# Row tiles transposed on TensorE, and a filtered spectrum laid out class by class

## The chip, the core and the metric

The kernel runs on one core of a Trainium2 chip. The metric is device time in microseconds (us) from start to end of one execution; lower is better. Its engines are TensorE (PE, matrix multiplication into PSUM; its loads of weights are listed as PEld), VectorE (DVE), ScalarE (ACT), GpSimd (POOL) and SyncE (SP), whose queue issues nearly all DMAs here. They run side by side, and each works through its own list in order.

## The reference

A normalised input goes through two branches, whose results are added to the input. Branch A is a filter in the frequency domain (a real two-dimensional FFT over 2048 rows and 640 columns, a product with a complex filter, the inverse), branch B a gated linear unit.

```python
xn = _layernorm(x, axis=-1)                  # x: 1 x 2048 x 640, bf16
X = jnp.fft.rfft2(xn.astype(jnp.float32))    # 2048 x 321
y = jnp.fft.irfft2(X * (w_r + 1j * w_i), s=(2048, 640)).astype(jnp.bfloat16)
h = (xn @ w_gate) * (xn @ w_up)              # 2048 x 1536
out = x + y + h @ w_down
```

## The kernel before

The 2048 rows are taken as 16 tiles of 128 rows and 640 columns. Everything lies in one SBUF tensor, `arena`, and one PSUM tensor, `ps`, of eight banks; so the profile names only these two, and the stages are told apart by line.

- **Layer norm.** Each tile's mean and variance come either from DVE (two L754, then L761) or from ACT (a sum L736, a sum of squares L745); `act_set` and `act_stats` say which tile goes where. ACT takes the root (L770, L771), DVE the reciprocal (L778) and the scaling in place (L795, named `mul`).
- **Transposes.** The gated unit needs the rows with their columns on the partitions. Tiles 0 to 3 are transposed on PE, five 128x128 blocks each (L814, named `T0`), and copied out of PSUM by ACT or DVE (`eT0`; L681 and L682 are the lines of all such copies on ACT and on DVE). Tiles 4 to 15 are transposed by a DMA each (L802, `xt`).
- **Gated unit.** `GU` multiplies by gate and up weights: L973 for tiles 0 and 1 singly (128 columns) and 2 and 3 together (256), L951 for four tiles at once (512 columns, 440 matmuls). The results are copied out (L681, L682) and multiplied on DVE (L991, L993).
- **Forward FFT.** DVE's butterflies over the columns (L857 to L892, `S1` to `S5`) feed a matmul `R` (L905). Then `D` (L1034) transforms within classes of columns, which are residues modulo ten, paired into four classes and one more for the multiples of five; `C` (L1053) finishes the rows.
- **Filter.** `WM` multiplies the spectrum in PSUM by the filter's real and imaginary parts: four L1070 for the four classes and one L1073 for the fifth, for each of 16 steps. `SM` (L1086, L1087) combines the products. `JA` to `JD` (L682, L681, L1099, L1100) write copies with real and imaginary parts exchanged.
- **Inverse.** `IA` (L1116), `I` (L1144), butterflies `V1` to `V5` (L1168 to L1201), and `IV` (L1233), which adds into the same PSUM bank as the down product.
- **Down product.** `ACC` (L1221, 396 matmuls) accumulates the gated unit's output; L1260 and L1242 add the input, and the rows are stored.

The order is not made while the kernel runs. Every piece of work is a task with what it reads and writes, and a table, `_PLAN`, lists for every task its engine and PSUM bank. Each engine runs its tasks in the table's order, and waits are derived from the dependences and from who held the bank before. The numbers given to tasks as durations serve only that bookkeeping. PE begins with `nwarm` matmuls on constants (L714) while the first tile is loaded and normalised.

In the filtered spectrum `L`, each of four groups holds 640 elements in which a class's elements lie four apart, and `IA` reads its weights so:

```python
yl = v_l[:, lr, o_ + 128 + k:o_ + 640:4] if k < 4 else v_l[:, lr, o_:o_ + 128]
```

Of the kernel before, what the change touches and what calls it, by code (L numbers as in the profile page):

```python
# [255 lines left out]
def _build_tables():  # L256
    t = {}
# [7 lines left out]
    for tt in range(16):  # L265
        for g in range(_G):
            q = tt * _G + g
# [14 lines left out]
    b = np.arange(64)  # L282
# [18 lines left out]
    l_ = 5 * np.arange(65)  # L301
    e = np.exp(-1j * two_pi * ((b[:, None] * l_[None, :]) % _D) / _D)
    w = np.where((l_ == 0) | (l_ == 320), 1.0, 2.0)[:, None] / _D * np.conj(e).T
    for o in range(2):
        own = (l_ % 2 == o).astype(np.float64)
        fd[64 * o:64 * o + 64, 512:577] = e.real * own[None, :]
        fd[64 * o:64 * o + 64, 578:641] = (e.imag * own[None, :])[:, 1:64]
        gd[63:128, 512 + 64 * o:576 + 64 * o] = w.real * own[:, None]
        gd[0:63, 512 + 64 * o:576 + 64 * o] = -(w.imag * own[:, None])[1:64]
# [59 lines left out]
_LP = 321  # L369
_YS = 1090  # L370
# [30 lines left out]
def _d_act(n):  # L401
# [4 lines left out]
    (12, 1, -1), (19, 2, -1), (10, 0, 1), (0, 3, -1), (11, 4, -1), (13, 4, -1), (18, 2, -1), (20, 2, -1), (28, 2, -1),  # L406
    (27, 2, -1), (170, 1, -1), (14, 4, -1), (8, 3, -1), (21, 1, -1), (22, 2, -1), (29, 2, -1), (23, 2, -1), (30, 1, -1),
    (31, 2, -1), (32, 2, -1), (24, 0, 3), (25, 2, -1), (26, 2, -1), (9, 0, 7), (33, 0, 1), (34, 2, -1), (35, 2, -1),
    (181, 0, 0), (182, 2, -1), (36, 1, -1), (37, 1, -1), (15, 4, -1), (43, 1, -1), (38, 1, -1), (169, 4, -1), (179, 0, 6),
    (180, 2, -1), (39, 2, -1), (40, 2, -1), (183, 2, -1), (44, 1, -1), (45, 1, -1), (46, 2, -1), (47, 2, -1), (189, 0, 1),  # L410
    (191, 0, 0), (190, 1, -1), (192, 1, -1), (193, 2, -1), (172, 4, -1), (186, 0, 6), (171, 4, -1), (112, 2, -1), (187, 1, -1),
    (41, 0, 2), (42, 1, -1), (184, 0, 7), (185, 1, -1), (16, 4, -1), (54, 2, -1), (113, 2, -1), (48, 0, 6), (49, 1, -1),
    (62, 1, -1), (194, 0, 5), (196, 0, 3), (197, 1, -1), (195, 1, -1), (188, 2, -1), (198, 2, -1), (50, 2, -1), (51, 2, -1),
    (53, 2, -1), (114, 2, -1), (55, 2, -1), (52, 2, -1), (63, 1, -1), (206, 0, 2), (207, 1, -1), (64, 1, -1), (204, 0, 7),
    (205, 1, -1), (115, 2, -1), (173, 4, -1), (209, 0, 6), (174, 4, -1), (65, 1, -1), (210, 1, -1), (66, 1, -1), (67, 2, -1),
    (56, 1, -1), (57, 2, -1), (116, 2, -1), (199, 0, 3), (200, 1, -1), (70, 2, -1), (201, 0, 2), (202, 1, -1), (203, 2, -1),
    (58, 2, -1), (208, 2, -1), (17, 4, -1), (121, 2, -1), (72, 1, -1), (1, 4, -1), (211, 0, 7), (175, 4, -1), (212, 1, -1),
    (176, 4, -1), (177, 4, -1), (73, 1, -1), (117, 0, 2), (118, 1, -1), (119, 0, 5), (74, 1, -1), (213, 2, -1), (122, 2, -1),
    (68, 2, -1), (123, 2, -1), (75, 1, -1), (76, 1, -1), (77, 2, -1), (216, 0, 1), (217, 1, -1), (214, 0, 0), (215, 1, -1),
    (218, 2, -1), (221, 0, 2), (222, 1, -1), (78, 2, -1), (124, 2, -1), (219, 0, 3), (220, 1, -1), (223, 2, -1), (80, 2, -1),  # L420
    (224, 0, 4), (120, 1, -1), (225, 1, -1), (82, 1, -1), (60, 2, -1), (226, 0, 2), (227, 1, -1), (229, 0, 6), (230, 1, -1),
    (83, 1, -1), (84, 1, -1), (178, 4, -1), (231, 0, 5), (125, 2, -1), (128, 0, 6), (126, 0, 3), (129, 1, -1), (232, 1, -1),
    (228, 2, -1), (130, 2, -1), (233, 2, -1), (131, 2, -1), (59, 4, -1), (71, 4, -1), (2, 4, -1), (236, 0, 0), (237, 1, -1),
    (61, 4, -1), (85, 1, -1), (234, 0, 2), (127, 1, -1), (86, 1, -1), (235, 1, -1), (238, 2, -1), (132, 2, -1), (92, 1, -1),
    (241, 0, 6), (242, 1, -1), (239, 0, 7), (240, 1, -1), (93, 1, -1), (243, 2, -1), (133, 2, -1), (87, 2, -1), (246, 0, 4),
    (244, 0, 1), (245, 1, -1), (94, 1, -1), (247, 1, -1), (248, 2, -1), (134, 2, -1), (69, 4, -1), (249, 0, 6), (250, 1, -1),
    (95, 1, -1), (96, 1, -1), (97, 2, -1), (251, 0, 2), (252, 1, -1), (90, 2, -1), (253, 2, -1), (88, 2, -1), (98, 2, -1),
    (100, 2, -1), (254, 0, 7), (255, 1, -1), (256, 0, 3), (257, 1, -1), (438, 4, -1), (433, 4, -1), (259, 0, 4), (260, 1, -1),
    (258, 2, -1), (137, 0, 5), (139, 0, 0), (437, 4, -1), (435, 4, -1), (441, 4, -1), (472, 4, -1), (101, 4, -1), (91, 4, -1),
    (434, 4, -1), (470, 4, -1), (3, 4, -1), (135, 0, 2), (136, 1, -1), (143, 2, -1), (138, 1, -1), (102, 1, -1), (261, 0, 7),  # L430
    (262, 1, -1), (79, 4, -1), (89, 4, -1), (141, 0, 3), (269, 0, 2), (263, 2, -1), (142, 1, -1), (140, 1, -1), (266, 0, 5),
    (267, 1, -1), (144, 2, -1), (270, 1, -1), (264, 0, 4), (265, 1, -1), (268, 2, -1), (145, 2, -1), (271, 0, 5), (274, 0, 1),
    (103, 1, -1), (104, 1, -1), (272, 1, -1), (273, 2, -1), (81, 4, -1), (442, 4, -1), (466, 4, -1), (146, 2, -1), (105, 1, -1),
    (106, 1, -1), (275, 1, -1), (279, 0, 4), (280, 1, -1), (276, 0, 0), (277, 1, -1), (278, 2, -1), (107, 2, -1), (147, 2, -1),
    (110, 2, -1), (108, 2, -1), (468, 4, -1), (469, 4, -1), (281, 0, 6), (282, 1, -1), (286, 0, 7), (287, 1, -1), (283, 2, -1),
    (284, 0, 3), (152, 0, 4), (148, 0, 6), (153, 1, -1), (99, 4, -1), (431, 4, -1), (440, 4, -1), (432, 4, -1), (4, 4, -1),
    (683, 4, -1), (109, 4, -1), (111, 4, -1), (473, 4, -1), (156, 2, -1), (429, 4, -1), (439, 4, -1), (467, 4, -1), (471, 4, -1),
    (149, 1, -1), (285, 1, -1), (288, 2, -1), (157, 2, -1), (150, 0, 0), (289, 0, 2), (151, 1, -1), (154, 0, 4), (291, 0, 6),
    (296, 0, 0), (290, 1, -1), (292, 1, -1), (155, 1, -1), (293, 2, -1), (158, 2, -1), (301, 0, 2), (299, 0, 6), (300, 1, -1),
    (294, 0, 4), (295, 1, -1), (304, 0, 7), (306, 0, 6), (6, 4, -1), (297, 1, -1), (298, 2, -1), (159, 2, -1), (160, 2, -1),  # L440
    (305, 1, -1), (307, 1, -1), (309, 0, 0), (310, 1, -1), (302, 1, -1), (303, 2, -1), (311, 0, 7), (312, 2, -1), (308, 2, -1),
    (163, 0, 5), (164, 1, -1), (167, 0, 1), (161, 0, 3), (162, 1, -1), (168, 2, -1), (314, 0, 0), (315, 2, -1), (313, 2, -1),
    (165, 0, 4), (316, 0, 6), (317, 2, -1), (166, 1, -1), (446, 0, 2), (447, 1, -1), (448, 2, -1), (474, 0, 0), (443, 0, 4),
    (444, 2, -1), (445, 1, -1), (324, 0, 7), (325, 1, -1), (477, 0, 2), (479, 1, -1), (478, 2, -1), (318, 2, -1), (321, 0, 6),
    (322, 1, -1), (436, 4, -1), (451, 0, 4), (452, 2, -1), (475, 1, -1), (476, 1, -1), (449, 0, 2), (450, 2, -1), (498, 4, -1),
    (503, 4, -1), (504, 4, -1), (497, 4, -1), (534, 4, -1), (453, 2, -1), (319, 0, 7), (320, 1, -1), (323, 2, -1), (454, 2, -1),
    (326, 0, 6), (327, 1, -1), (328, 2, -1), (505, 0, 4), (506, 1, -1), (508, 0, 0), (509, 1, -1), (510, 1, -1), (331, 0, 7),
    (332, 1, -1), (334, 0, 2), (335, 1, -1), (329, 0, 6), (507, 1, -1), (482, 0, 0), (483, 2, -1), (480, 0, 2), (481, 2, -1),
    (484, 2, -1), (455, 1, -1), (330, 1, -1), (341, 0, 7), (342, 1, -1), (336, 0, 4), (337, 1, -1), (456, 3, -1), (457, 3, -1),
    (460, 0, 5), (462, 0, 6), (463, 1, -1), (458, 0, 0), (464, 0, 7), (465, 1, -1), (461, 1, -1), (344, 0, 1), (345, 1, -1),  # L450
    (536, 0, 6), (459, 1, -1), (537, 1, -1), (339, 0, 2), (538, 1, -1), (340, 1, -1), (349, 0, 1), (532, 4, -1), (500, 4, -1),
    (499, 4, -1), (502, 4, -1), (501, 4, -1), (511, 0, 3), (333, 2, -1), (485, 2, -1), (531, 4, -1), (565, 4, -1), (535, 4, -1),
    (560, 4, -1), (530, 4, -1), (528, 4, -1), (529, 4, -1), (513, 0, 6), (351, 0, 0), (486, 2, -1), (350, 1, -1), (352, 1, -1),
    (512, 2, -1), (567, 0, 1), (568, 1, -1), (569, 1, -1), (346, 0, 5), (347, 1, -1), (487, 3, -1), (488, 3, -1), (489, 0, 4),
    (490, 1, -1), (514, 2, -1), (338, 2, -1), (515, 2, -1), (354, 0, 0), (355, 1, -1), (539, 0, 2), (540, 1, -1), (541, 1, -1),
    (493, 0, 1), (491, 0, 6), (492, 1, -1), (494, 2, -1), (356, 0, 4), (357, 1, -1), (359, 0, 7), (360, 1, -1), (517, 2, -1),
    (343, 2, -1), (516, 2, -1), (495, 0, 2), (5, 4, -1), (430, 4, -1), (533, 4, -1), (544, 0, 0), (594, 4, -1), (561, 4, -1),
# [887 lines left out]
```

## Time and profile before

| what | value |
|---|---|
| median of 3 runs (lowest to highest) | 196.71 us (196.61 to 196.75) |
| the profiled execution | 196.57 us |
| its span, first to last instruction | 194.9 us |
| PE busy | 190.9 us, 98% |
| DVE busy | 176.7 us, 91% |
| ACT busy | 136.4 us, 70% |
| POOL busy | 12.2 us, 6% |
| mean DMA rate | 122 GB/s, 23.73 MB |
| DMA transposes | 12, issued 19.6 to 58.6 us, 3.8 us median to landing |
| chain that ended last | PE 95%, DVE 2%, DMA 1%, ACT 1% |

The profile is of one execution. A group row gives line, engine, operation, what is written from what, the shape and the count; after the bar, the busy time of the group, the mean duration of one in ns, and the idle time of the engine before it. A matmul's recorded end is modelled and overlaps the next, so the time from one start to the next says more than a duration. The chain follows, from the last instruction back, what each step waited for.

### The profile page before, as it was taken

What the parts mean: (1) busy time and instruction counts of PE and PEld (TensorE: products, weight loads), DVE (VectorE), ACT (ScalarE), POOL (GpSimd) and SP (SyncE); (2) the same over time, 40 slices, a digit from 0 to 9 for tenths busy, and PEclk for the clock granted to TensorE, in tenths of its full rate; (3) what the DMA queues carried; (4) which work ended last, traced back from release to release, by engine and by line L of the source; (5) the groups of instructions that cost most, each with busy time, mean ns of one, the idle gap of its engine ahead of it and who ended that gap; (6) DMA issues with size and microseconds to landing.
All of it is one profiled execution on the core that took longest, in us unless ns stands there. A gap on an engine that the chain in (4) does not pass through costs nothing.

```text
span 194.9 us, 4074 instructions
## 1 busy us (share of the span) xinstructions
PE 190.9 (98%) x1568; PEld 120.5 (62%) x1568; DVE 176.7 (91%) x369; ACT 136.4 (70%) x275; POOL 12.2 (6%) x22
## 2 busy tenths in 40 slices
PE   8899999999999999999999999999999999999995
PEld 8797454454454565555655555557777777777774
DVE  3899999999999999999989999987999999999713
ACT  3899999999884679989999999667305523253130
POOL 1000000000000000331031221120000000000000
DMA  5999974016869921366465510005001543135412
GB/s 173 324 370 324 214 98 111 0 37 105 155 130 222 258 68 27 96 145 193 118 153 135 153 36 31 3 0 170 4 0 53 144 143 104 40 95 172 134 68 67
DMA packets 29666, 23.73 MB, mean 122 GB/s; under 512 B 10448, under 2 KB 27600, under 8 KB 29520
## 3 DMA queue, kind: packets, MB, share of 16 engines
q1 hardware_dynamic: 28848, 23.08, 46.5%
q10 hardware_dynamic: 800, 0.41, 0.7%
q8 instruction: 12, 0.20, 0.5%
q14 instruction: 6, 0.05, 0.1%
HBM read 18.89 MB, written 2.62 MB: 110 GB/s over the span
## 4 chain that ended last, share of the span: by engine, by line
PE 95%; DVE 2%; DMA 1%; ACT 1%; issue 0%
PE ps L951 48%; PE ps L1221 27%; PE ps L973 5%; PE ps L1116 3%; PE ps L1034 2%; PE ps L1053 2%; PE ps L905 2%; PE ps L1144 2%; PE ps L1233 2%; DMA arena<-in_A_x_dram 1%; DVE arena L754 1%; PE ps L814 1%; ACT arena L681 1%; DVE arena L682 0%; DVE arena L761 0%
## 5 line engine op out<-in xcount | busy, mean ns | idle before, releaser
L681 ACT ACTIVATE arena<-ps 128x512 bf16<-128x512 f32 (+5 forms) x211 | 111.3, 582 | 48.8 <-PE ps L1233 13.8
L951 PE MATMUL ps<-arena 128*128 128x512 bf16 x440 | 101.9, 379 | 0.0
L951 PEld LDWEIGHTS ps<-arena 128*128 128x128 bf16 x440 | 40.9, 98 | 43.1 <-ACT arena L681 0.9
L1221 PE MATMUL ps<-arena 128*128 128x320 bf16 (+2 forms) x396 | 57.2, 295 | 0.0
L1221 PEld LDWEIGHTS ps<-arena 128*128 128x128 bf16 x396 | 37.6, 98 | 13.2
L1070 DVE TENSOR_TENSOR arena<-ps,arena 128x256 bf16<-128x256 f32 x64 | 22.6, 414 | 1.5 <-PE ps L1053 1.3
L991 DVE TENSOR_TENSOR arena<-arena 128x512 bf16<-128x512 bf16 x44 | 18.7, 426 | 0.6 <-ACT arena L681 0.2
L1260 DVE TENSOR_TENSOR arena<-arena 128x640 bf16<-128x640 bf16 x15 | 7.0, 486 | 5.4 <-ACT arena L681 5.4
L682 DVE CAST arena<-ps 128x512 bf16<-128x512 f32 (+4 forms) x16 | 10.1, 639 | 1.5 <-PE ps L973 0.4
L745 ACT ACTIVATE arena<-arena 128x640 bf16<-128x640 bf16 x12 | 10.2, 849 | 0.1
L682 POOL COPY arena<-arena 64x252 bf16<-64x252 bf16 x8 | 4.1, 510 | 92.8 <-DVE arena L1087 92.5
L973 PE MATMUL ps<-arena 128*128 128x128 bf16 (+1 forms) x120 | 9.5, 237 | 0.3 <-DVE arena L682 0.3
L1116 PEld LDWEIGHTS ps<-arena 128*128 128x128 bf16 x160 | 7.9, 116 | 3.0
L736 ACT ACTIVATE arena<-arena 128x640 bf16<-128x640 bf16 x12 | 9.0, 753 | 0.2
L973 PEld LDWEIGHTS ps<-arena 128*128 128x128 bf16 x120 | 8.4, 98 | 1.1 <-issue 0.4
L1100 POOL TENSOR_SCALAR arena<-arena 64x252 bf16<-64x252 bf16 x8 | 7.5, 943 | 22.9 <-DVE arena L1087 22.6
L1116 PE MATMUL ps<-arena 128*128 128x64 bf16 x160 | 8.3, 198 | 0.0
L1233 PE MATMUL ps<-arena 128*128 128x320 bf16 (+2 forms) x33 | 8.3, 295 | 0.0
L1034 PEld LDWEIGHTS ps<-arena 128*128 128x128 bf16 x160 | 6.4, 98 | 2.7 <-issue 0.5
L857 DVE TENSOR_TENSOR arena<-arena 128x768 f32<-128x768 bf16 (+1 forms) x10 | 7.9, 789 | 0.0
L1073 DVE TENSOR_TENSOR arena<-ps,arena 128x260 bf16<-128x260 f32 x16 | 6.9, 432 | 0.0
L1034 PE MATMUL ps<-arena 128*128 128x64 bf16 (+1 forms) x160 | 6.9, 193 | 0.0
(61 smaller groups left out, 184.3 us busy)
## 6 DMA issues: line engine op xcount, KB each, us to landing
arena<-in_A_x_dram SPq DMA_DIRECT2D x19, 160.0 KB, 2.6
arena<-in_A_w_i_dram SPq DMA_DIRECT2D x30, 80.2 KB, 2.3
arena<-in_A_w_r_dram SPq DMA_DIRECT2D x30, 80.2 KB, 2.3
out_dram<-arena SPq DMA_DIRECT2D x15, 160.0 KB, 1.9
arena<-in_B_w_gate_dram SPq DMA_DIRECT2D x4, 320.0 KB, 6.5
arena<-in_A_x_dram SPq DMA_DIRECT2D x1, 1280.0 KB, 10.8
arena<-c_tf SPq DMA_DIRECT2D x4, 256.0 KB, 4.6
arena<-c_ti SPq DMA_DIRECT2D x2, 512.0 KB, 5.0
```

What stands on the lines that cost most here:

```text
L681: return c.e.activation(dst, src, _ACTF.Copy)
L682: return c.e.tensor_copy(dst, src)
L736: return c.e.activation(v_jk, v_x[:, b, :], _ACTF.Copy, scale=1.0 / _D, accum_out=v_m32[:, b:b + 1])
L745: return c.e.activation(v_jk, v_x[:, b, :], _ACTF.Square, scale=-1.0, bias=v_m32[:, b:b + 1], accum_out=v_ss[:, b:b + 1])
L951: ins = c.e.matmul(ps[:, bk, :], v_gw[:, w, j, ft, :], v_xt[:, j, rows], start=(j == 0), stop=(j == 4))
L973: ins = c.e.matmul(ps[:, bk, i * n:(i + 1) * n], v_gw[:, w, j, ft0 + i, :], v_xt[:, j, rows], start=(j == 0), stop=(j == 4))
L991: return c.e.tensor_tensor(v_ht[:, ft0, rows], gb[:, 0, :], gb[:, 1, :], _OP.mult)
L1034: ins = c.e.matmul(ps[:, bk + i, k * 64:k * 64 + n], v_uq[:, k, t + i, :], v_fd[:, k * 128 + w * n: k * 128 + w * n + n], start=True, stop ...
L1070: c.e.tensor_tensor(dst, xh, wv, _OP.mult)
L1116: ins = c.e.matmul(ps[:, bk, 64 * k:64 * k + 64], yl, v_ti[:, q, 0, :], start=True, stop=True)
L1221: ins = c.e.matmul(ps[:, bk, 0:sl3.stop - sl3.start], v_ht[:, ft, a * 128:(a + 1) * 128], v_wd[:, ft, sl3], start=(ft == _FT_ORDER[0]), st ...
L1233: return c.e.matmul(ps[:, bank_of(own), 0:sl3.stop - sl3.start], v_sm[:, 2, :], v_v[:, a, sl3], start=False, stop=True)
```

## The change

1. The branch that issued a DMA transpose is gone; all 16 tiles go through `T0` and `eT0`. That makes 60 more 128x128 matmuls on PE, nine more tile copies on ACT, three more on DVE and twelve DMAs fewer on SP.
2. The products and the filtered spectrum are laid out class by class. In the products every class has a row of `_LB` = 66 elements, so that L1070 writes neighbouring results 66 elements apart. In `L` every class has 128 contiguous elements, which `IA` reads as they lie. The combine runs over 20 rows of 66 instead of four of 321; the two unused elements at the end of a row are cleared once by POOL. The fifth class's table in the inverse is reordered to match.
3. Tile 1's statistics go to ACT and tile 2's to DVE, `nwarm` is 43 instead of 42, and `_PLAN` is a new table. The constants' load for `R` stands earlier in SP's queue; of the inverse's copies out of PSUM four move from ACT to DVE; the order of tasks on each engine is new throughout.

```diff
+_LB = 66
...
 _PLAN = (
...
-        b_pr = alloc("PR", 8 * 321)
-        b_l = alloc("L", 2 * 2624)
+        b_pr = alloc("PR", 8 * 5 * _LB)
+        b_l = alloc("L", 2 * 2560)
...
-        v_pr = V("PR").rearrange("p (w g n) -> p w g n", w=2, g=4)
-        v_l = V("L").rearrange("p (r n) -> p r n", r=2)
+        v_pr = V("PR").rearrange("p (w g b c) -> p w g b c", w=2, g=4, b=5)
+        v_l = V("L").rearrange("p (r g b c) -> p r g b c", r=2, g=4, b=5)
...
-        nwarm = opts.get("nwarm", 42)
+        nwarm = opts.get("nwarm", 43)
...
-        aset = set(opts.get("act_set", (2, 3))) | set(range(opts.get("act_stats", 6), 16))
+        aset = set(opts.get("act_set", (1, 3))) | set(range(opts.get("act_stats", 6), 16))
...
-                if b >= opts.get("xt_dma", 4):
-                    def em_xt(c, b=b):
-                        return c.e.dma_start_transpose(v_xt[:, :, b * 128:(b + 1) * 128], v_x[:, b, :])
-                    T("xt%d" % b, "sp", 1330.0, em_xt, reads=[(b_x, ("s", b, b + 1))],
...
-                    continue
...
-                        dst = v_pr[:, w, 2 * pb:2 * pb + 2, 65:321].rearrange("p g (h m k) -> p h g m k", h=2, k=4)[:, h]
+                        dst = v_pr[:, w, 2 * pb:2 * pb + 2, 1:5, 32 * h:32 * h + 32].rearrange("p g k m -> p g m k")
                         c.e.tensor_tensor(dst, xh, wv, _OP.mult)
...
-                d5 = v_pr[:, :, 2 * pb:2 * pb + 2, 0:65]
+                d5 = v_pr[:, :, 2 * pb:2 * pb + 2, 0, 0:65]
                 return c.e.tensor_tensor(d5, x5, wt[:, :, :, 0:321:5], _OP.mult)
+            if t == 0:
+                def em_pad(c):
+                    return c.e.memset(v_pr[:].rearrange("p w g b c -> p (w g b) c")[:, :, 64:_LB], 0.0)
+                T("pad", "pool", 300.0, em_pad, writes=[(b_pr, None)], prio=pq - 0.002)
...
-                pa_, pb_ = v_pr[:, 0], v_pr[:, 1]
-                l_ = v_l[:, lr, 63:2623].rearrange("p (g n) -> p g n", g=4)[:, :, 0:321]
+                pa_, pb_ = (v_pr[:, w].rearrange("p g b c -> p (g b) c") for w in range(2))
+                l_ = v_l[:, lr].rearrange("p g b c -> p (g b) c")[:, :, 0:_LB]
...
-                src = l0[:, :, 1:64] if five else l0[:, :, 65:321]
-                dst = l1[:, :, 0:63] if five else l0[:, :, 321:577]
+                src = v_l[:, lr, :, 0, 1:64] if five else v_l[:, lr, :, 1:5, 0:64]
+                dst = v_l[:, lr, :, 0, 65:128] if five else v_l[:, lr, :, 1:5, 64:128]
...
-                        yl = v_l[:, lr, o_ + 128 + k:o_ + 640:4] if k < 4 else v_l[:, lr, o_:o_ + 128]
+                        yl = v_l[:, lr, q % 4, (k + 1) % 5]
```

## The prediction

> **What bounds the kernel now.** I read the page's busy shares first, then the chain that ended last in order of time, then the waits of TensorE (PE).
>
> ```profile
> PE 190.9 (98%) x1568; PEld 120.5 (62%) x1568; DVE 176.7 (91%) x369; ACT 136.4 (70%) x275; POOL 12.2 (6%) x22
> ```
>
> ```profile
> 40.67 0.84 PE ps L905 x15
> ...
> 42.87 10.79 PE ps L951 x50
> ...
> 75.10 0.59 PE ps L1034 x20
> ...
> 81.64 0.67 PE ps L1116 x20
> ...
> 138.95 6.66 PE ps L1221 x49
> ```
>
> A busy share alone proves little, because matmuls overlap. The chain rows (start us, length us, what) give the step from one matmul to the next: 10.79/50 = 0.216 us for 512 columns, 6.66/49 = 0.136 for 320, 0.84/15 = 0.056 for 128. These lie on one line (0.416 ns a column), so each is a rate and not a wait in disguise. With these steps, from L973's start at 7.31 us to the end of the last matmul (about 192.5), I add up: L951 440 x 0.2158 = 94.95; L1221 372 x 0.136 + 12 x 0.0825 + 12 x 0.056 = 52.3; L1233 4.3; L973 80 x 0.056 + 40 x 0.109 = 8.8; L814 0.6; L905 4.5; L1144 4.5; L1034 160 x 0.0296 = 4.7; L1053 32 x 0.137 = 4.4; L1116 160 x 0.0335 = 5.4. That is 184.4 us of matmul in a stage of 185.2 us. **PE's own work is the bound; only 0.8 us of waiting is left in it.** PE's listed waits all end by 7.31. DVE is full too, but beside PE:
>
> ```profile
> 10.00:60.00 50.00, 50.00 (x330) 27.60 (x328) 49.96 (x110) 46.11 (x104) 0.00 (x0) 1.00 0.71 155
> 60.00:130.00 70.00, 69.91 (x605) 38.26 (x604) 66.70 (x148) 61.57 (x110) 11.63 (x16) 1.00 0.44 110
> ```
>
> Columns: window, then busy PE, PEld, DVE, ACT, POOL, the granted clock (1.00), DMA. Spare are 3.9 us of ACT in the first window, 3.3 of DVE and 8.4 of ACT in the second.
>
> **The change part by part.** The profiled execution took 196.57 us (span 194.9 and 1.7 around it), 0.14 below the median of the runs, 196.71; I add the terms to 196.71.
>
> *Twelve tiles transposed on PE.* The old four show the price:
>
> ```profile
> 10.10 0.44 PE L814 MATMUL ps<-arena 128*128 128x128 bf16 x5
> 10.38 0.72 PE L973 MATMUL ps<-arena 128*128 128x128 bf16 x10
> ...
> 10.94 0.44 PE L814 MATMUL ps<-arena 128*128 128x128 bf16 x5
> ...
> 11.22 3.46 PE L973 MATMUL ps<-arena 128*128 128x128 bf16 x40
> ```
>
> PE goes on 0.28 us after each group of five starts: 12 x 0.28 = **+3.36 us**, all on the bound. No gap can hide it, since only 0.8 us of gaps exist. The Trainium skill ("TensorE: Matmul & The Clock Gate", Part 4) gives about 275 ns for one transpose in a kernel and says that the full clock does not engage for it. By that the sixty would be 16.5 us and the estimate 212.8; the rows above, 56 ns each, decide against it.
>
> They add waits to PE's queue: each group waits for its tile's scaling on DVE (L795), and ready GLU matmuls (L951) stand behind it. The first, tile 6, is the tightest: DVE ends group 0's butterflies at about 16.5 us (5.5 us of rows L857 to L892 and two 0.2 products from 10.4), then four statistics 1.6, aggregates and reciprocals 0.3, three scalings 1.1 and two products 0.7 make 20.2. PE reaches it at 12.65 + 4.36 (L973) + 3 x 1.08 (L951) + 2 x 0.28 (L905) = 20.8. So it waits for nothing, by 0.6.
>
> What leaves is twelve transposing DMAs (L802, 1.2 to 2.6 us each on SP's queue, 3.8 us median to landing). PE never waited for them, so this gains nothing; the filter loads that were queued behind them start earlier, which no PE wait asks for either.
>
> *Their evictions.* Nine more 640-element bf16 evictions on ACT and three on DVE. ACT's two of before took 0.72 each, 0.58 start to start: 9 x 0.58 = 5.3 us. Between 10 and 70 us ACT has 3.9 + 3.4 = 7.3 spare, so they fit, closely. On DVE 3 x about 0.4 = 1.2 in a stretch with none spare; but the class stage (L1034) also starts later by the PE time put ahead of it (eleven groups, 3.1 us), and that is room for the butterflies that feed it. Nothing on the path; if the cover fails, PE waits for a bank or for normalised rows (rival C).
>
> *Class by class layout.* The inverse matmul L1116 read its weights in steps of four elements; now they are contiguous. Same matmul size, contiguous weights: L1034.
>
> ```profile
> L1116 PEld LDWEIGHTS ps<-arena 128*128 128x128 bf16 x160 | 7.9, 116 | 3.0
> ...
> L1034 PEld LDWEIGHTS ps<-arena 128*128 128x128 bf16 x160 | 6.4, 98 | 2.7 <-issue 0.5
> ```
>
> The chain gives 33.5 ns a matmul against 29.5: 160 x 4 ns = **-0.64 us**. Ends: 0 and -0.64; I take the latter, as L1034 differs in nothing else that the rows show.
>
> The products are on DVE:
>
> ```profile
> 72.73 1.41 DVE L1070 TENSOR_TENSOR arena<-ps,arena 128x256 bf16<-128x256 f32 x4
> 74.05 0.43 DVE L1073 TENSOR_TENSOR arena<-ps,arena 128x260 bf16<-128x260 f32 x1
> ```
>
> Until now L1070 wrote runs of four neighbouring elements; now each element is written 66 from the last. No row of before writes so. Nearest: L1070 itself reads PSUM 64 elements apart, and L1073 reads its filter five apart. Both lie on the line of the f32 copies (256 elements 414 ns, 260 432, 512 689: about 1.02 ns an element), so hopping reads cost nothing; I take **0** for hopping writes. The slowest nearby row is POOL's copy, 510 ns for 252 elements, 2.02 ns each: +1.0 x 256 x 64 = 16.4 us of DVE as the upper end; the lower end, two elements a cycle as in L991 (512 in 426 ns), -8 us, off the path. Here the skill speaks against the change: "Vector Engine (DVE) Microarchitecture Reference", section 5.2, measures 1.71 to 2.51 ns a column instead of 1.05 where only the output hops every element, on 4-byte words. For 256 x 64 columns that would be 10.8 to 23.9 us of DVE, by estimate, and the end at 209 to 222. No row here shows a hopping write, so this stays open.
>
> The combines (L1086, L1087) grow from 1284 to 1320 elements: 16 x 0.02 = 0.3 us of DVE. The mirror copies keep their 1024 elements. One POOL memset clears the pad; it must come after the last butterfly (R's last matmul, 68 us) and before the first product (72.7), 4 us for a small memset. Four inverse evictions move from ACT to DVE, 4 x 0.49 = 1.9 us of the 3.3 spare. Nothing on the path.
>
> *New order, start.* Tile 1's statistics go from DVE to ACT, and tile 2's come back.
>
> ```profile
> 4.18 0.21 DVE L761 BATCH_NORM_AGGREGATE arena<-arena 128x2 f32<-128x12 f32 x1
> 4.37 0.89 DVE L754 BATCH_NORM_STATS2 arena<-arena 128x6 f32<-128x320 bf16 x2
> 4.42 0.29 ACT L771 ACTIVATE arena<-arena 128x1 f32<-128x1 f32 x1 [1.34 <-DVE arena L761]
> ...
> 5.18 0.15 DVE L778 RECIPROCAL arena<-arena 128x1 f32<-128x1 f32 x1
> ```
>
> Tile 0's reciprocal waited for tile 1's statistics from 4.71 to 5.18. Now it starts at 4.75, and the first transpose at 5.45 instead of 5.87 (the 43 warming matmuls end at 0.84 + 43 x 0.107 = 5.44). Evicted in 0.55, tile 0 feeds its first ten L973 at 6.9. But tile 1 is later: two ACT passes from 4.75 (tile 2's took 1.78), then root to scaling 0.98: its transpose starts at 7.56, before 6.57. PE does ten matmuls meanwhile, then tile 1's group, then ten more to 8.41, and waits 0.3 for tile 1's evictions (behind a 0.48 statistic of tile 2), to 8.73. Then 20 matmuls (1.12), tile 3's group, 20, tile 2's group, 20: the first 256-column matmul starts at 12.65, where it was 12.34 with the same work behind it. **+0.3 us**; ends -0.5 (the early start kept) and +1.0 (tile 1's delay uncovered).
>
> Sum: 196.71 + 3.36 - 0.64 + 0.3 = **199.7 us**.
>
> **Rivals.** *B: the hopping writes make DVE the bound.* Of 3.3 us spare, 1.9 + 0.3 are used; what 1.1 leaves over 64 products is 17 ns each, and from there on the end moves. At POOL's price, 16.4 - 1.1 = 15.3 later: 215. For it: no row of before writes this way. Against: both hopping reads are free. *C: evictions in 10 to 70 us come late.* ACT keeps only 2 us; if a quarter to half of the 6.5 added us is uncovered, PE stalls 1.5 to 3: 201 to 203. Against: before, PE lost 0.8 us with ACT at 92% and DVE at 100%. *D, the other side: the transposes cost PE nothing*, being absorbed where matmuls only seem back to back. Then 196.71 - 0.64 + 0.3 = 196.4, not slower. It decides when the sixty cost less than 0.64 - 0.3 + 0.39 (0.2% of the time) = 0.73 us, 12 ns each instead of 56. For it: the busy share counts modelled ends. Against: the straight line through three widths, and 184.4 of 185.2.
>
> **How the numbers follow.** Forecast 0.80, B 0.09, C 0.07, D 0.04, half of it faster and half within the bound. Range: low end 196.71 + 3.36 - 0.64 - 0.5 - 0.8 (all old waits gone) = 198.1; high end 196.71 + 3.36 + 0 + 1.0 and half of C's least stall = 201.8, widened into C to 202.3. About 0.2% is what a measurement can tell from no change: faster 0.02, same 0.02, slower 0.96.
>
> **What would show it.** Twelve more L814 groups with PE going on after 0.28 us; L1116 at 29.5 ns a matmul; products still about 1.68 us for five; PE's waits after 13 us under 1 us; the last matmul about 3 us later. I am wrong if products take over 1.8 us for five, if transposes step by other than 56 ns, or if PE's waits list names ACT or DVE for more than a microsecond.

## The result, and the profile after

| | before | after |
|---|---|---|
| median (lowest to highest) | 196.66 us (196.42 to 196.75) | 256.83 us (256.16 to 259.01) |
| ratio, 95% interval | | 1.308 (1.300 to 1.317) |
| profiled execution, span | 196.57, 194.9 us | 256.16, 254.4 us |

Runs more than 1.5% longer than the fastest of their kernel are left out of its time; two profiles below, of the new layout alone and of the busier TensorE, are of such runs.

The kernel became 60 us slower, where 3 had been forecast. That the direction came out right says little for the forecast: the reason given for it, the transposes, makes some 3 of the 60 us, and the rest comes from a term that had been taken at nothing.

The page of the kernel after: busy shares, the granted clock in 40 slices, the chain by engine, and groups (busy us, mean ns of one, idle us before and what ended it).

```profile
PE 209.9 (82%) x1611; PEld 126.8 (50%) x1629; DVE 231.1 (91%) x375; ACT 142.1 (56%) x281; POOL 12.1 (5%) x23
...
PEclk9999999999997986889579788979599999999999
...
PE 60%; DVE 36%; ACT 1%; issue 1%; DMA 1%; ACTq 0%
...
L946 PE MATMUL ps<-arena 128*128 128x512 bf16 x422 | 113.3, 414 | 4.0 <-DVE arena L1068 2.7
L1065 DVE TENSOR_TENSOR arena<-ps,arena 128x256 bf16<-128x256 f32 x64 | 75.5, 1462 | 3.8 <-PE ps L1048 3.8
...
L1112 PE MATMUL ps<-arena 128*128 128x64 bf16 x160 | 10.0, 204 | 27.3 <-DVE arena L1068 18.3
...
L1029 PE MATMUL ps<-arena 128*128 128x64 bf16 (+1 forms) x160 | 8.2, 206 | 8.3 <-DVE arena L1068 8.3
```

Line numbers have moved by a few: the product L1070 is now L1065 (L1073 is L1068), GU is L946, D L1029, C L1048, IA L1112, T0 L809. Read the page in three steps. PE's share fell from 98% to 82% and DVE's stayed at 91%, of a span 60 us longer: DVE has 231.1 us of work where it had 176.7. One group accounts for nearly all of that: 64 products that took 22.6 us take 75.5. (L946 shows 422 of its 440 matmuls; the records of 18 are missing.) And PE's idle time now names its releaser: the inverse (L1112) and the class transform (L1029) wait for the products.

The chain that ended last, in order of time (start us, length us, what):

```profile
20.82 0.56 PE ps L809 x10
21.38 2.16 PE ps L946 x10
...
74.06 0.29 PE ps L1048 x2
74.37 4.73 DVE arena L1065 x4
79.10 0.26 DVE arena L1068
79.36 4.62 DVE arena L1065 x4
83.97 0.27 DVE arena L1068
84.27 0.84 DVE arena L1085
85.12 0.85 DVE arena L1086
```

Up to 74 us the chain runs along PE, and the transposes stand in it as forecast, 0.28 us for five. Then it changes to DVE: five products take 4.89 to 4.99 us, where they took 1.68. Start to start a product takes 1.14 us instead of 0.33. In sixteen steps that is 16 x (4.94 - 1.68) = 52 us.

Windows of the kernel after (window, busy PE, PEld, DVE, ACT, POOL, granted clock, DMA):

```profile
10.00:73.00 63.00, 62.57 (x466) 36.28 (x472) 62.49 (x131) 57.37 (x122) 0.17 (x1) 1.00 0.39 117
73.00:188.00 115.00, 75.22 (x524) 36.20 (x533) 108.52 (x133) 55.64 (x97) 11.35 (x16) 0.82 0.21 53
188.00:253.00 65.00, 64.14 (x523) 46.98 (x522) 54.80 (x95) 22.74 (x49) 0.00 (x0) 1.00 0.28 89
```

Nearly all of the loss lies in the middle window, where products are made: 115 us for what took about 58 before (72.7 to some 131 us). PE is idle for 40 us there, and in that window the clock granted to it is 0.82; before and after it is 1.00.

### The profile page after: what moved, and what is told of

Same layout as the page of the kernel before. It is cut to its first block, busy times and chain, and to the rows that moved or that the text cites. A ratio compares the mean times of both kernels' runs of the same rounds, so it can differ in the third digit from the quotient of the medians.

```text
span 254.4 us, 4173 instructions
## 1 busy us (share of the span) xinstructions
PE 209.9 (82%) x1611; PEld 126.8 (50%) x1629; DVE 231.1 (91%) x375; ACT 142.1 (56%) x281; POOL 12.1 (5%) x23
## 4 chain that ended last, share of the span: by engine, by line
PE 60%; DVE 36%; ACT 1%; issue 1%; DMA 1%; ACTq 0%
DVE arena L1065 29%; PE ps L946 27%; PE ps L1217 21%; PE ps L968 3%; PE ps L1140 2%; PE ps L900 2%; PE ps L1229 2%; DVE arena L1068 2%; PE ps L809 2%; DVE arena L986 1%; PE ps L1112 1%; DVE arena L1086 1%; DVE arena L1085 1%; DMA arena<-in_A_x_dram 1%; DVE arena L684 1%
## 5 line engine op out<-in xcount | busy, mean ns | idle before, releaser
L683 ACT ACTIVATE arena<-ps 128x512 bf16<-128x512 f32 (+6 forms) x217 | 115.7, 585 | 100.1 <-PE ps L946 31.1
L946 PE MATMUL ps<-arena 128*128 128x512 bf16 x422 | 113.3, 414 | 4.0 <-DVE arena L1068 2.7
L1065 DVE TENSOR_TENSOR arena<-ps,arena 128x256 bf16<-128x256 f32 x64 | 75.5, 1462 | 3.8 <-PE ps L1048 3.8
L946 PEld LDWEIGHTS ps<-arena 128*128 128x128 bf16 x440 | 43.1, 104 | 49.8 <-issue 11.4
L1217 PEld LDWEIGHTS ps<-arena 128*128 128x128 bf16 x396 | 37.7, 98 | 13.4
L1112 PE MATMUL ps<-arena 128*128 128x64 bf16 x160 | 10.0, 204 | 27.3 <-DVE arena L1068 18.3
L1112 PEld LDWEIGHTS ps<-arena 128*128 128x128 bf16 x160 | 8.1, 105 | 36.1 <-DVE arena L1068 22.7
L1029 PE MATMUL ps<-arena 128*128 128x64 bf16 (+1 forms) x160 | 8.2, 206 | 8.3 <-DVE arena L1068 8.3
L684 DVE CAST arena<-ps 128x320 bf16<-128x320 f32 (+3 forms) x19 | 11.7, 631 | 2.6 <-PE ps L946 1.1
L1029 PEld LDWEIGHTS ps<-arena 128*128 128x128 bf16 x160 | 7.0, 107 | 12.1 <-DVE arena L1068 7.8
L1068 DVE TENSOR_TENSOR arena<-ps,arena 128x260 bf16<-128x260 f32 x16 | 10.1, 632 | 0.0
L1097 POOL TENSOR_SCALAR arena<-arena 64x252 bf16<-64x252 bf16 x8 | 7.3, 916 | 52.1 <-DVE arena L1086 51.7
L968 PEld LDWEIGHTS ps<-arena 128*128 128x128 bf16 x120 | 8.4, 98 | 1.4 <-issue 0.7
L1048 PE MATMUL ps<-arena 128*128 128x321 bf16 x32 | 7.2, 320 | 0.5 <-DVE arena L1086 0.3
```

Of the source, the lines that this page charges most:

```text
L683: return c.e.activation(dst, src, _ACTF.Copy)
L684: return c.e.tensor_copy(dst, src)
L946: ins = c.e.matmul(ps[:, bk, :], v_gw[:, w, j, ft, :], v_xt[:, j, rows], start=(j == 0), stop=(j == 4))
L968: ins = c.e.matmul(ps[:, bk, i * n:(i + 1) * n], v_gw[:, w, j, ft0 + i, :], v_xt[:, j, rows], start=(j == 0), stop=(j == 4))
L1029: ins = c.e.matmul(ps[:, bk + i, k * 64:k * 64 + n], v_uq[:, k, t + i, :], v_fd[:, k * 128 + w * n: k * 128 + w * n + n], start=True, stop ...
L1065: c.e.tensor_tensor(dst, xh, wv, _OP.mult)
```

## The experiments

Theory: writing each product 66 elements from the last makes DVE the bound. Rivals: the new order or the sixty transposes; or any step over the arrays, on the reading side as well.

### Parts of the change alone

**Old layout put back; transposes, new table and start kept** (run twice, on two chips):

```diff
-  dst = v_pr[:, w, 2 * pb:2 * pb + 2, 1:5, 32 * h:32 * h + 32].rearrange("p g k m -> p g m k")
+  dst = v_pr[:, w, 2 * pb:2 * pb + 2, 65:321].rearrange("p g (h m k) -> p h g m k", h=2, k=4)[:, h]
...
-  yl = v_l[:, lr, q % 4, (k + 1) % 5]
+  yl = v_l[:, lr, o_ + 128 + k:o_ + 640:4] if k < 4 else v_l[:, lr, o_:o_ + 128]
```

> The changed kernel with the old layout of products and spectrum put back (writes in runs of four, the inverse's weights read at step four); transposes on TensorE, new table and start stay. Theory (the 66-element writes made the 60 us): the terms of the forecast without the layout's, 196.7 + 3.36 + 0.3 = 200.3 us, five products back at 1.68 us a step. Rival (the new order or the sixty transposes made it): within a few us of 256.8.

Measured: 201.11 us (200.36 to 202.03), ratio 1.023 (1.019 to 1.027). The second time 201.04 us (200.87 to 201.13), ratio 1.0226 (1.021 to 1.024). The page of the second, then its products, then a window of the first:

```profile
PE 194.0 (97%) x1629; PEld 123.5 (62%) x1629; DVE 179.4 (90%) x375; ACT 140.3 (70%) x281; POOL 12.1 (6%) x23
```

```profile
L1065 DVE TENSOR_TENSOR arena<-ps,arena 128x256 bf16<-128x256 f32 x64 | 22.6, 413 | 1.4 <-PE ps L1048 1.4
```

```profile
10.00:72.00 62.00, 62.00 (x470) 35.83 (x468) 61.52 (x130) 56.39 (x121) 0.10 (x1) 1.00 0.38 116
```

The products are back at 413 ns. So 56 of the 60 us go with the layout. Transposes and order cost 4.45 us, against 3.66 in the forecast.

**The new layout alone** (DMA transposes, old table):

```diff
-  dst = v_pr[:, w, 2 * pb:2 * pb + 2, 65:321].rearrange("p g (h m k) -> p h g m k", h=2, k=4)[:, h]
+  dst = v_pr[:, w, 2 * pb:2 * pb + 2, 1:5, 32 * h:32 * h + 32].rearrange("p g k m -> p g m k")
```

> The kernel before, with the new layout alone (DMA transposes, old table; the pad is cleared by VectorE inside the first product step). Theory: 16 steps x 3.27 us of products more on VectorE, less what was spare there (3.3 us), and 0.64 off the inverse matmuls: 196.7 + 52.3 - 3.3 - 0.6 = 245 us, more if TensorE, waiting, runs at a lower granted clock. Rival (order or transposes): 196 to 197 us.

Measured: 253.2 us, and 258.3 in the profiled execution, whose page reads:

```profile
PE 212.0 (83%) x1568; PEld 125.3 (49%) x1568; DVE 228.4 (89%) x371; ACT 139.0 (54%) x275; POOL 12.1 (5%) x22
...
L1074 DVE TENSOR_TENSOR arena<-ps,arena 128x256 bf16<-128x256 f32 x64 | 75.6, 1465 | 10.3 <-PE ps L1054 10.3
```

The layout alone makes the loss, without the transposes and with the old order. The same products cost the same, 1465 ns. The 253.2 us, a single run, is 8 us above the 245 of the theory, so the products' work less the spare time is not the whole of it (see the account below).

### Which step costs

**Same places, walked row by row.** The loops over class and position change places, so each product writes 32 neighbours before it hops; the filter is read ten apart instead.

```diff
-  xh = ps[:, bk:bk + 2, 0:256].rearrange("p g (k h m) -> p h g m k", k=4, h=2)[:, h]
-  wv = wt[:, w, :, 0:320].rearrange("p g (m k) -> p g m k", k=10)
+  xh = ps[:, bk:bk + 2, 0:256].rearrange("p g (k h m) -> p h g k m", k=4, h=2)[:, h]
+  wv = wt[:, w, :, 0:320].rearrange("p g (m k) -> p g k m", k=10)
...
-  dst = v_pr[:, w, 2 * pb:2 * pb + 2, 1:5, 32 * h:32 * h + 32].rearrange("p g k m -> p g m k")
+  dst = v_pr[:, w, 2 * pb:2 * pb + 2, 1:5, 32 * h:32 * h + 32]
```

> The changed kernel with one thing altered: each product walks a class's row from end to end (32 neighbours written, then the next class), where it went from class to class at every element. Same elements, same places, same layout; the filter is now read at step ten and PSUM without a step. Theory (lone writes cost, stepped reads do not): five products at about 1.7 us and a total of 199.7 us, the forecast itself. Rival 1 (any step over the arrays costs, on the reading side too): products stay near 4 ns an element, total near 257. Rival 2 (layout harmless, order at fault): near 257 with products at 1.7 us.

Measured: 212.31 us (212.25 to 212.36), ratio 1.080 (1.078 to 1.082).

```profile
PE 196.8 (93%) x1629; PEld 122.3 (58%) x1629; DVE 191.6 (91%) x375; ACT 141.3 (67%) x281; POOL 12.1 (6%) x23
...
L1065 DVE TENSOR_TENSOR arena<-ps,arena 128x256 bf16<-128x256 f32 x64 | 34.9, 608 | 0.6 <-PE ps L1048 0.5
```

Neither side was right. 44.5 us come back, so the write was the main thing; but the product takes 608 ns and not 414. The filter is now read ten apart, and the next runs show that such a read alone costs as much (605). So the forecast's argument that hopping reads are free fails here too.

**Steps one by one.** Behind the last work of the kernel before, products of 256 elements were added, five of a kind, each waiting for the last. For example:

```diff
+  bench(lambda: eng.tensor_tensor(lone(sc, 4), s0, s1, _OP.mult))      # write 4 apart
+  bench(lambda: eng.tensor_tensor(runs(sc, 66, 2), sr[2][0], sr[2][1], _OP.mult))
+  bench(lambda: eng.tensor_tensor(sc[:, 0:256], s0, lone(fl, 10), _OP.mult))   # read 10 apart
```

> The kernel before, and after its last VectorE instruction 125 more products of 256 elements, five of each pattern of write or read, each waiting for the one before; their results are not used, and the total says nothing. Looked for is the time of one by its step. Theory L (a lone bf16 write costs by distance, not by count of runs): step 2 and 4 stay near 414 ns, from some distance on 1140; at that price runs of two 66 apart take about half of 1140, runs of four about a quarter and so no more than 414. Theory C (the changing of direction, four classes in turn, costs): one lone step of 66 stays near 414 and only the four-way patterns take 1140. Theory W (it is the two-byte word that costs): the same patterns with f32 results stay near 414; if not, they cost like bf16.

> As the first series of steps, 115 further products of five each behind the end of the kernel before; the total says nothing. Theory P (VectorE writes in words of four bytes, and half a word costs): aligned pairs 66 apart take 424 ns as they did, pairs that start at an odd element take at least 1290; lone elements at step 3, 5 and 6 lie between 443 and 1290 in step with their distance, and 128 lone elements take about half of 1290. Rival R (only the number of runs counts): odd pairs stay at 424 as well. Reads: the filter's step of five stays at 424, step 10 was 603; the edge between them is looked for, and whether a step in PSUM costs. The three walks of the kernel's own products are put side by side: about 424, 1290, 605.

Groups of the first series, mean ns behind the bar. In order: lone bf16 written 66 apart, 8 apart, 4 apart; f32 written 33 apart; the filter read 10 apart; lone bf16 2 apart; pairs 66 apart.

```profile
L1323 DVE TENSOR_TENSOR arena<-ps,arena 128x256 bf16<-128x256 f32 x5 | 6.4, 1287 | 0.2
...
L1319 DVE TENSOR_TENSOR arena<-ps,arena 128x256 bf16<-128x256 f32 x5 | 6.4, 1289 | 0.2
...
L1318 DVE TENSOR_TENSOR arena<-ps,arena 128x256 bf16<-128x256 f32 x5 | 3.6, 724 | 0.2
...
L1336 DVE TENSOR_TENSOR arena<-ps,arena 128x256 f32<-128x256 f32 x5 | 3.1, 611 | 0.2
...
L1339 DVE TENSOR_TENSOR arena<-ps,arena 128x256 bf16<-128x256 f32 x5 | 3.0, 605 | 0.2
...
L1317 DVE TENSOR_TENSOR arena<-ps,arena 128x256 bf16<-128x256 f32 x5 | 2.2, 443 | 0.2
...
L1331 DVE TENSOR_TENSOR arena<-ps,arena 128x256 bf16<-128x256 f32 x5 | 2.1, 425 | 0.2
```

Of the second series: the kernel after's own walk; lone bf16 written 66 apart with both sources in SBUF; pairs 66 apart that begin at an odd element; 128 lone elements 66 apart; whole rows; the filter read 6 and 5 apart; the kernel before's own walk; 256 neighbours with both sources in SBUF; 128 neighbours.

```profile
L1338 DVE TENSOR_TENSOR arena<-ps,arena 128x256 bf16<-128x256 f32 x5 | 6.5, 1292 | 0.2
L1348 DVE TENSOR_TENSOR arena<-arena 128x256 bf16<-128x256 bf16 x5 | 6.4, 1290 | 0.2
...
L1333 DVE TENSOR_TENSOR arena<-ps,arena 128x256 bf16<-128x256 f32 x5 | 4.3, 866 | 0.2
L1335 DVE TENSOR_TENSOR arena<-ps,arena 128x128 bf16<-128x128 f32 x5 | 3.6, 723 | 0.2
...
L1339 DVE TENSOR_TENSOR arena<-ps,arena 128x256 bf16<-128x256 f32 x5 | 3.0, 604 | 0.2
...
L1343 DVE TENSOR_TENSOR arena<-ps,arena 128x256 bf16<-128x256 f32 x5 | 2.4, 485 | 0.2
...
L1342 DVE TENSOR_TENSOR arena<-ps,arena 128x256 bf16<-128x256 f32 x5 | 2.1, 429 | 0.2
...
L1337 DVE TENSOR_TENSOR arena<-ps,arena 128x256 bf16<-128x256 f32 x5 | 2.1, 424 | 0.2
...
L1349 DVE TENSOR_TENSOR arena<-arena 128x256 bf16<-128x256 bf16 x5 | 1.5, 292 | 0.2
L1336 DVE TENSOR_TENSOR arena<-ps,arena 128x128 bf16<-128x128 f32 x5 | 1.5, 291 | 0.2
```

All steps, in ns for 256 elements:

| step in elements | 1 | 2 | 3 | 4 | 5 | 6 | 8 | 10 | 16 | 66 |
|---|---|---|---|---|---|---|---|---|---|---|
| bf16 written singly | 424 | 443 | 584 | 724 | 866 | 1007 | 1289 | | 1225 | 1287 |
| filter (bf16) read | 424 | 424 | | 424 | 429 | 485 | 598 | 605 | 606 | |

The write's price rises by some 141 ns for each element of step beyond two, up to eight elements, and is flat from there; steps of 32 to 80 lie between 1227 and 1296, and 96 alone (run in the four-class walk only) is dearer, at 1432. Going from class to class or straight on makes no difference (1293 against 1287), so theory C falls. Theory L is right that distance counts, but not in its sizes: step four already takes 724 where some 414 was expected, and pairs cost nothing extra where half of 1140 was. Theories W and P hold in part. An aligned pair is free and one that begins at an odd element is not (so rival R falls), but it takes 866 where theory P said at least 1290; f32 words 33 apart, the same distance in bytes, still cost 611; and lone bf16 two apart cost almost nothing. The free pairs do fit the f32 price: taking off the 158 ns that neighbours have beyond 256 x 1.04, a lone f32 word takes (611 - 158) / 256 = 1.8 ns, and 128 pairs at that price would take less than 256 neighbours do (an estimate). These are prices by pattern; what in the engine makes them is not shown. A read costs far less than a write, begins to cost between five and six, and lies near 605 from eight to sixteen; at 40 it takes 679. A step of two or four in PSUM costs nothing (424).

From 128 to 256 lone elements, (1287 - 723) / 128 = 4.4 ns an element; neighbours take (424 - 291) / 128 = 1.04. That is the kernel's figure: 1140 ns for 256 is 4.45 ns each.

**Half of the products hopping:**

```diff
+  if w == 1:
+      xh, wv, dst = (v.rearrange("p g m k -> p g k m") for v in (xh, wv, dst))
```

> The changed kernel with the products of the imaginary filter part (two of the four L1065 of a step) walking whole rows, those of the real part hopping as in the change. Theory (VectorE is the bound and the total follows its busy time one for one): from 212.3 (all whole rows, 608 ns each) with 32 products dearer by 731 less 194 ns start to start, 1140 against 525: 32 x 0.615 = 19.7 us more, so 232 us at a full clock; if TensorE's granted clock falls while it waits, VectorE also waits for the row matmuls L1048, by up to the 3.8 us seen in the changed kernel: 232 to 236. Rival (the loss has a threshold and does not go with the work): near 212 or near 257.

Measured: 231.39 us (231.35 to 231.42).

```profile
PE 197.0 (86%) x1611; PEld 122.1 (53%) x1629; DVE 209.0 (91%) x375; ACT 141.6 (62%) x281; POOL 12.1 (5%) x23
```

The theory's 232 us is met, and there is no threshold: the time goes with DVE's work.

**Pairs, in the kernel before:**

```diff
+  for g in range(2):
+      xh = ps[:, bk + g, 0:256].rearrange("p (k h a b) -> p h a k b", k=4, h=2, b=2)[:, h]
+      wv = wt[:, w, g, 0:320].rearrange("p (a b k) -> p a k b", k=10, b=2)
...
+      dst = v_pr[:, w, 2 * pb + g, 1:5, 32 * h:32 * h + 32].rearrange("p k (a b) -> p a k b", b=2)
```

> The kernel before with the new layout, and each product walked in pairs: two neighbours of a class, then the next class, so that each write fills an aligned word of four bytes. One pattern cannot say that for two groups at once, so a step has eight products of 128 elements in place of four of 256. Theory (pairs are written freely): 8 x about 0.2 us against 4 x 0.33 start to start, 0.27 us a step and 4.3 us in all on VectorE, against 3.3 us that were spare; less 0.5 on TensorE: 196.2 to 197.5 us. If the filter's reads (pairs ten apart, back and forth) cost as step ten did, 0.7 ns an element more: 8 us or so above that.

Measured: 199.36 us (199.07 to 199.65), ratio 1.014 (1.013 to 1.016).

```profile
PE 191.8 (97%) x1568; PEld 118.8 (60%) x1568; DVE 181.1 (92%) x435; ACT 137.1 (69%) x275; POOL 12.1 (6%) x22
...
L1075 DVE TENSOR_TENSOR arena<-ps,arena 128x128 bf16<-128x128 f32 x128 | 26.9, 283 | 0.1
```

The pairs behave as expected, 198 ns start to start for 128 elements, and the filter's reads in pairs cost nothing. DVE's work grew by the 4.3 us forecast. But the 3.3 us of spare time did not absorb it: against 196.59 - 0.5 the end is 3.3 us later, so only about 1 us was absorbed, and the forecast of 196.2 to 197.5 us is missed. This is the best form of the new layout that was run, and it is slower than the kernel before.

### TensorE's side

**The transposes of tiles 4 to 15 repeated**, two and four times:

```diff
-  for j in range(5):
+  for j in [0, 1, 2, 3, 4] * (4 if b >= 4 else 1):
```

> The old layout with transposes on TensorE, and the transposes of tiles 4 to 15 done twice each, 60 more 128x128 matmuls whose results are the same. Theory (each group costs its 0.28 us on the bound and nothing hides it): 201.1 + 3.36 = 204.5 us. Rival (the transposes lie in gaps; what the old layout still has above the kernel before comes from the order): near 201.1.

> The same kernel as the one with the old layout put back, to stand beside the next one on the same chip: by the forecast's terms 200.3 us, by its first measurement 200.4 to 202.0.

> The old layout, and the transposes of tiles 4 to 15 done four times each: 180 more 128x128 matmuls with the same results. Doubling them had cost 2.2 us where 3.36 was expected, with a scatter of 1.7 us in the kernel it is compared with. Theory (0.28 us a group, all on the bound): 10.1 us above the single transposes of the same chip, 210 to 211. Rival (a third of each group is absorbed in waits): about 6.6 us above, 207 to 208.

Measured: twice, 203.33 us (203.22 to 203.86), 2.2 above the single ones, which ran on another chip; four times, 210.02 us (209.94 to 210.36), 8.98 above the single ones of the same chip (201.04). The second is the better lever: 8.98 / 180 = 50 ns a matmul, 0.25 us a group. The rival's 207 to 208 us is out: little of a group is hidden.

**The inverse's weights as neighbours, in the kernel before:**

```diff
-  yl = v_l[:, lr, o_ + 128 + k:o_ + 640:4] if k < 4 else v_l[:, lr, o_:o_ + 128]
+  yl = v_l[:, lr, o_ + 128 + 128 * k:o_ + 256 + 128 * k] if k < 4 else v_l[:, lr, o_:o_ + 128]
```

> The kernel before, with one change: the inverse's weights are taken as 128 neighbours instead of every fourth element. The wrong elements are read, so the result of branch A is not the reference's; all else is as before. Theory (the term of 0.64 us): 29.5 instead of 33.5 ns a matmul and 196.6 - 0.64 = 195.9 us. Rival: the step is in TensorE's queue elsewhere and the total stays at 196.6.

Measured: 196.2 against 196.7 us, ratio 0.9975 (0.9966 to 0.9985): -0.5 us, between 0.3 and 0.7.

**TensorE kept busier in the slow stage:**

```diff
-  for k in range(5):
+  for k in [0, 1, 2, 3, 4] * 4:
       yl = v_l[:, lr, q % 4, (k + 1) % 5]
```

> The changed kernel with every inverse matmul of L1112 issued four times (480 more, the same results): 480 x 29 ns = 13.9 us more on TensorE inside the stage in which it waits some 40 us for VectorE. Theory (VectorE's busy time is the bound there): the added matmuls cost at most what VectorE then waits for them, 0 to 3 us: 256.8 to 260. Theory plus clock (the low granted clock of that stage, 0.82 on the mean, comes from TensorE's waiting, and costs the 3.3 us by which VectorE waits longer for L1048): a higher granted clock, and 253 to 257. Rival (TensorE still sets the end): 256.8 + 13.9 = 271 us.

Measured: 255.23 and 258.03 us, within about 1 us of the scatter of the kernel after (256.16 to 259.01). From the page and the DVE waits (us, times, longest) of the profiled execution, which took 260.76:

```profile
L1112 PE MATMUL ps<-arena 128*128 128x64 bf16 x640 | 24.5, 198 | 23.4 <-DVE arena L1068 16.5 <-issue 6.9
```

```profile
DVE arena L1065 <- PE ps L1048: 4.5, 5, 1.6
```

Of 13.9 us of added matmul nothing clear of the scatter reached the end: PE is not the bound of this stage. The mean clock over the span rose from 0.90 to 0.92 in the runs of the kernel after to 0.95 to 0.96 here. Whether the low clock has a price, this does not settle: the mean of the two times, 256.6 us, lies at the edge of both forecasts, and the wait for L1048, 4.5 us against 3.8, is from a longer execution.

### The account

If DVE's work decides, an edit of the layout should end later by what it adds to DVE's busy time, less 0.5 us of near weights. "Expected" below is that sum, from the base's time and the pages' busy times.

| kernel | base | DVE busy | expected | measured |
|---|---|---|---|---|
| whole rows | old layout, 201.04, DVE 179.4 | 191.6 | 212.7 | 212.31 |
| half hopping | the same | 209.0 | 230.1 | 231.39 |
| the kernel after | the same | 231.1 | 252.2 | 256.83 |
| pairs | before, 196.59, DVE 176.7 | 181.1 | 200.5 | 199.36 |
| layout alone | before, 196.56, DVE 176.7 | 228.4 | 247.8 | 253.2 |

Up to 30 us of added work the end follows the sum within 1.3 us. With all products hopping it does not quite: the layout alone is 5.4 us above the sum, the kernel after 4.6; in the profiled executions the span grew by 254.4 - 199.3 = 55.1 us, 51.7 of it DVE's work and 3.4 idle time of DVE, which its waits name: for L1048 3.8 us where the old layout had 1.4, for L1112 1.0 where it had 0.5, for L946 1.1 where it had 0.6. The new order is not needed for this, since the layout alone has it with the old one; whether PE comes late because of its lower clock stays open.

## Why the prediction was wrong

- **The failed step: "so hopping reads cost nothing; I take 0 for hopping writes".** The measured term is 64 x (1140 - 331) ns = 51.8 us of DVE, and with it DVE, not PE, bounds the stage in which products are made. Three things were wrong in the step. A read was taken for a write: eight elements apart, a bf16 read costs 0.7 ns an element more than neighbours and a bf16 write 3.4. And the reads did not show what was read out of them: L1073 reads five apart, the last step before the price begins (429, then 485 at six), and L1070's 64 apart are in PSUM, where the steps tried are free. Last, L1070 did not write "runs of four": by its index it wrote 128 neighbours in a row for each group, so no product of before hopped in its writes at all. (The 414 ns set among the f32 copies is L1070's own row; a copy of 256 takes 426. The line through them holds all the same.)
- **The upper end** came from POOL's copy, another engine: 16.4 us, a third of the truth. Ends taken from the nearest row held nothing, because no row of the profile shared the property in question. "No row here shows a hopping write" was a sentence about how little was known, and 0.09 was too small a chance for rival B, whose mechanism it was.
- **The page weighed against it pointed the right way.** The Trainium skill, "Vector Engine (DVE) Microarchitecture Reference", section 5.2, gave 1.71 to 2.51 ns a column for a hopping output of four-byte words. The f32 run lies in that range, at the 1.8 ns worked out above. For bf16 the same sum gives 4.4, so the 10.8 to 23.9 us worked out from the page were less than half of what came. "Advanced Engine Details and Errata", SBUF Cachelines, speaks of 16-byte lines and a penalty when each access meets another line; both rows of the table level off at about eight bf16 elements, which is 16 bytes, but the writes' price begins at three.
- **Rival B's threshold was too high.** 17 ns a product rested on 1.1 us left of DVE's 3.3 spare. The pairs spent 4.4 us and lost 3.3, whole rows spent 12.2 and lost about 11.8. So idle time summed over a window is not all usable. Why so little of it was used is not shown; a likely reason is that it lies where DVE waits, and that each late product makes PE wait at its own step.
- **The rest held.** Transposes: 56 ns by the chain, 50 by repetition, 3.0 to 3.4 us of the 3.36. Near weights: 29 ns a matmul, -0.5 us for -0.64. Combines: 842 ns for 824, as sized. Start: the first matmul of 256 columns at 12.50 us instead of 12.34, +0.16 for +0.3. Rivals C and D are out: with the old layout PE is busy 62.00 of the 62 us from 10 to 72, which leaves no room for C's stall of 1.5 to 3 us, and the transposes cost about what they take.
- With the old layout 0.8 us more was lost than forecast, 4.45 for 3.66. In one profile PE waits 1.0 us at L1048, in the other, 0.8 us shorter, it does not; what makes that wait was not followed further.
- The signs named beforehand did show it: "products take over 1.8 us for five" (4.9) and PE's waits naming DVE for more than a microsecond (29 us).

## What to carry to other kernels

Look at where an instruction writes before where it reads: single two-byte elements written three or more apart cost VectorE up to three times a contiguous write here, and over four times where both sources were bf16 in SBUF, while aligned pairs cost nothing, so let a layout change write aligned pairs or leave it. If an engine at 91% gets a new access pattern that no row of the profile shows, its price is unknown and not zero: multiply the worst price known for any such pattern by the count first, and see whether the bound would move. A saving of 0.5 us on the bound does not pay for a pattern repeated 64 times on its neighbour.

## What was not expected of the hardware

- A lone bf16 write 132 bytes from the last takes 4.4 ns, an f32 write at the same distance 1.8, and a pair of bf16 no more than neighbours do. With both sources in SBUF the 256 lone bf16 take the same 1290 ns, against 292 for neighbours.
- Pairs that begin at an odd element take 866 ns against 424.
- While TensorE waited for VectorE its granted clock was 0.82 over 115 us, and 1.00 once it was busy again. The share of idle time alone does not set it: TensorE was busy 65% of those 115 us; with half of the products hopping it was busy 64.1 of the 92 us from 73 to 165, 70%, and the clock was 0.98; with the added matmuls of L1112 it was busy 80.6 of 115 us, 70% too, and the clock was 0.90.
